# Two groups' transposes moved to the DMA queue in a fused retention and feed-forward kernel, with a state update placed earlier and the last output cut in two

## The chip, the cores and the metric

The kernel runs on one core of one Trainium2 chip. The metric is the device time of one execution in microseconds (us). A core has five engines that run side by side, each through its own instructions in order: TensorE (PE in the profile, with its weight loads shown apart as PEld), VectorE (DVE), ScalarE (ACT), GpSimd (POOL) and SyncE (SP). SP computes nothing here: it issues the DMAs that bring inputs in, take outputs away and transpose tiles, one after the other, and 16 DMA engines carry them out.

## The reference

Two stages follow each other. The first is retention: attention without a softmax, whose scores are damped by the distance of the two positions, with one decay rate for each of 8 heads. The second is a feed-forward block on all 4608 tokens with the activation h·cos(h).

```
# q, k, v: (8 batches, 8 heads, 576 positions, 64), float32
scores = (1 / sqrt(64)) * q @ k^T
gamma  = 1 - 2 ** (-5 - head)
D[i,j] = gamma ** (i - j)  where i >= j, else 0
x      = (scores * D) @ v          # then to (4608 tokens, 512)
h      = x @ w_in                  # w_in: (512, 2048)
out    = (h * cos(h)) @ w_out      # w_out: (2048, 512)
```

## The kernel before, in words

**Groups.** The 4608 tokens are 36 groups of 128, numbered from 0, so the fourth group is group 3 and the seventh and eighth are groups 6 and 7. Nine groups are two batches; group 4 of every nine lies half in one batch and half in the next. Each group goes through these steps:

- `load(g)`: SP issues one DMA each for q, k and v (line 107), 256 KB each, in pieces of 256 bytes; a group that lies in two batches takes six DMAs of half the size.
- `prep(g)`: GpSimd multiplies q and k with powers of the decay and casts them to bf16 in the tile `qks` (lines 132 and 133), and casts v to `vb` (line 139). For group 3, k is done by VectorE, and the first four groups have v cast by ScalarE (line 158), behind a copy of their transposes.
- `transposes(g)`: `qks` turned by 128x128 blocks, into `qkT`. For groups below `N_PE_T` this is done by 8 TensorE instructions into PSUM (line 151) and two ScalarE copies out of it (line 156); for later ones it is one DMA that SP issues (line 146).
- `scores(g)`: 8 products of k and q (line 173), which need `qkT`, then masked by VectorE into `ret` (line 182).
- `state(g)`: 4 products of k and v that add to a running state (line 201), which need `qks` and `vb` but no transpose; VectorE brings it out as `sb` (line 210) for the next group.
- `attn_out(g)`: what the state gives (line 230) and what the scores give (line 243), summed in PSUM and evacuated to the tile `xT` (line 255).

**Blocks.** The feed-forward part runs in ten blocks n = 0 to 9 of 512, 256, 256 and then 512 tokens. In a block `mm1` makes h (line 270); ScalarE takes the cosine (line 278), VectorE the product (line 279). Then `mm2` multiplies with `w_out`, 16 instructions for each 128 tokens (line 287); ScalarE copies the result to `ot` (line 296) and SP issues its store (line 298).

**The order.** All orders are written out by hand. The attention work of later groups is put between the matmuls of `mm2` by the list `todo`: a pair (index, work) is done before the matmul of that index. `pair(6, "ab", 16, 27)` in block 1 means: state(6) before index 11, scores(6) and scores(7) before 16, state(7) before 21, attn_out of both before 27. Block 0's first `mm1` piece holds state(3) and attn_out(3) in its middle, before its fourth quarter.

After every store the function `feed(s)` (s is the output's group number) puts more work into the queues of SP and GpSimd: first the DMA transposes of the groups prepared by earlier feeds, then the loads of up to two more groups, then the preparation of up to two more. What a feed gives SP stands in SP's queue behind the store of s and ahead of the store of s + 1. Feed 0 loads groups 6 and 7; feed 1 loads 8 and 9; feed 2 issues the first DMA transpose (group 8) and loads 10 and 11; feed 3 issues the transposes of 9 and 10, feed 4 of 11 and 12, feed 5 of 13 and 14, and feeds 6, 7 and 8 of 15, 16 and 17. The loads of groups 4 and 5 wait for the second of the four `w_out` loads. Input tiles have 6 buffers each, `qks`, `vb` and `qkT` 8, and `ot` 4.

The last 128 tokens' output is cut by columns (`cols`), so that the first columns can be stored while the last are still computed.

Of the kernel before, what the change touches and what calls it, by code (L numbers as in the profile page):

```python
# [17 lines left out]
def kernel(  # L18
# [34 lines left out]
    widths = [512, 256, 256] + [512] * 7  # L53
    assert sum(widths) == NTOK
    starts = [sum(widths[:n]) for n in range(len(widths))]
    N_PE_T = 8

    consts = ctx.enter_context(tc.tile_pool(name="consts", bufs=1))
    first = ctx.enter_context(tc.tile_pool(name="first", bufs=1))
# [130 lines left out]
    def state(g):  # L190
        c = g % PER
        if c == PER - 1:
            return
        qks, vb, qkT, qT = tiles["a", g]
        fresh = c in (0, MIX)
        if fresh:
            tiles["stps"] = psum.tile([P, HG, P], F32, tag="st", name="st")
        ps = tiles["stps"]
        p0 = HP if c == MIX else 0
        for hg in range(HG):  # L200
            nc.tensor.matmul(  # L201
                ps[:, hg, :],
                lhsT=qks[p0:, 1, 2 * hg : 2 * hg + 2, :].rearrange("s h d -> s (h d)"),
                rhs=vb[p0:, 2 * hg : 2 * hg + 2, :].rearrange("s h d -> s (h d)"),
                start=(fresh and hg == 0),
                stop=(c in (MIX - 1, PER - 2) and hg == HG - 1),
                skip_group_check=True,
            )
        sb = stp.tile([P, HG, P], BF16, tag="sb", name="sb")
        nc.vector.tensor_tensor(  # L210
            out=sb,
            in0=ps,
            in1=diag2.unsqueeze(1).to_broadcast([P, HG, P]),
            op=ALU.mult,
        )
        tiles["sb", g + 1] = sb

    def attn_out(gs, bank, evac=nc.vector.tensor_copy):


        ps = psum.tile([P, len(gs), HG, P], F32, tag=bank, name="ov")
        for x, g in enumerate(gs):
            c = g % PER
            if c == 0:
                continue
            qT = tiles["a", g][3]
            sb = tiles.pop(("sb", g))
            n = HP if c == MIX else P
            for hg in range(HG):
                nc.tensor.matmul(  # L230
                    ps[:, x, hg, :n],
                    lhsT=sb[:, hg, :],
                    rhs=qT[:, hg, :n],
                    start=(hg == 0),
                    stop=False,
                    skip_group_check=True,
                )
        for x, g in enumerate(gs):
            vb = tiles.pop(("a", g))[1]
            ret = tiles.pop(("ret", g))  # L240
            for hg in range(HG):
                for he in range(2):
                    nc.tensor.matmul(  # L243
                        ps[he * D : he * D + D, x, hg, :],
                        lhsT=vb[:, 2 * hg + he, :],
                        rhs=ret[:, he, hg, :],
                        start=(g % PER == 0 and hg == 0),
                        stop=(hg == HG - 1),
                        skip_group_check=True,
                    )  # L250
        n = max(m for m in range(len(starts)) if starts[m] <= gs[0] * P)
        if ("x", n) not in tiles:
            tiles["x", n] = xp.tile([P, DG, 512], BF16, tag="xT", name="xT")
        t0 = gs[0] * P - starts[n]
        evac(  # L255
            tiles["x", n][:, :, t0 : t0 + len(gs) * P].rearrange("p c (x i) -> p x c i", i=P), ps
        )
# [23 lines left out]
    def mm2(n, tsi, et, c0=0, c1=DM):  # L281
        gT = tiles["g", n]
        if et == 0:
            bank = {0: "nmnm", 1: "nm", 2: "mn"}.get(n, "mnan")[tsi] if c0 == 0 else "ba"[c0 % DM // P % 2]
            tiles["o", tsi] = psum.tile([P, c1 - c0], F32, tag=bank, name="o")
        ps = tiles["o", tsi]
        nc.tensor.matmul(  # L287
            ps,
            lhsT=gT[:, et, tsi * P : (tsi + 1) * P],
            rhs=w_out_sb[:, et, c0:c1],  # L290
            start=(et == 0),
            stop=(et == ET - 1),
        )
        if et == ET - 1:
            ot = op.tile([P, c1 - c0], F32, tag="o", name="ot")
            nc.scalar.copy(ot, ps)  # L296
            s = starts[n] // P + tsi
            nc.sync.dma_start(out[s * P : (s + 1) * P, c0:c1], ot)  # L298
            feed(s)
# [98 lines left out]
    for g in range(G4):  # L398
        if g == 0:
            prep(1, early=True)  # L400
        w_dma += [load_w_in(e, e + 512) for e in ((0,), (512,), (1024, 1536), ())[g]]
        if g == 2:
            w_dma += [load_w_out(e, e + 4) for e in range(0, ET, 4)]
            load(4, gate=w_dma[5])
            load(5)
            nc.gpsimd.tensor_copy(tri_mix, tri)
            nc.gpsimd.memset(tri_mix[:HP, HP:], 0.0)
        if g + 1 < G4:
            state(g)
            transposes(g + 1, "nn", only=(1,))  # L410
            if g + 2 < G4:
                prep(g + 2, early=True)
            scores(g + 1, "ab"[(g + 1) % 2], idle=3)
            attn_out([g], "m", evac=nc.scalar.copy)
# [21 lines left out]
    for n, w in enumerate(widths):  # L436

        if n in (0, 3):
            halves = [(h, et) for et in range(0, ET, 4) for h in range(2)]
            if n == 3:  # L440
                halves.sort()
            blocks = [(et, half * 256, 256) for half, et in halves]
        elif n == 1:
            blocks = [(et, half * P, P) for half in range(2) for et in (0, 8)]
        else:
            blocks = [(et, 0, w) for et in range(0, ET, 1024 // w)]
        banks = {0: "abmabmab", 1: "amba", 2: "bmab", 3: "mamabmab"}.get(n, "abmabmab")
        for i, (et, c0, cw) in enumerate(blocks):

            inside = {  # L450
                (0, 0): {3: lambda: (state(3), attn_out([3], "m"))},
                (1, 0): {4: lambda: scores(5, "b")},
                (1, 1): {3: lambda: attn_out([5], "b", evac=nc.scalar.copy)},
            }.get((n, i), {})
            mm1(n, et, c0, cw, banks[i], inside)
            if (n, i) == (3, 1):
                late.pop()()

        g = starts[n] // P + w // P
        if n == 0:  # L460
            todo = [
                (45, lambda: transposes(4, "ab")),
                (49, lambda: state(4)),
                (50, lambda: scores(4, "a")),
                (57, lambda: attn_out([4], "a")),
                (61, lambda: transposes(5, "ba")),
                (63, lambda: state(5)),
            ]
        elif n == 1:
            todo = [(4, lambda: transposes(6, "mb")), (9, lambda: transposes(7, "mb"))]  # L470
            todo += pair(6, "ab", 16, 27)
        elif n == 2:
            todo = pair(g, "ab", 11, 24) + pair(g + 2, "ba", 31, 40)[:2]
            late += [lambda: (state(g + 3), attn_out([g + 2, g + 3], "b"))]
        elif n + 1 < len(widths):
            todo = [
                (5, lambda: state(g)),
                (12, lambda: scores2(g)) if n == 3 else (0, lambda: None),
                (25 if n == 3 else 20, lambda: (attn_out([g, g + 1], "m"), scores2(g + 2))),
                (16, lambda: state(g + 1)),  # L480
                (36, lambda: state(g + 2)),
                (52, lambda: (attn_out([g + 2, g + 3], "m"), scores2(g + 4))),
                (45, lambda: state(g + 3)),
            ]
        else:
            todo = []
        todo.sort(key=lambda u: u[0])
        order, cols = [], [(0, DM)]
        for tsi in range(w // P):
            if (n + 1, tsi + 1) == (len(widths), w // P):  # L490
                cols = [(0, DM // 2), (DM // 2, 3 * DM // 4), (3 * DM // 4, DM)]
            order += [(tsi, et, c0, c1) for c0, c1 in cols for et in range(ET)]
        if n == 0:

            part = 3 * ET // 4
            order[: 2 * ET] = [
                (tsi, et, 0, DM)
                for tsi, et in [(t, e) for e in range(part) for t in range(2)]
                + [(t, e) for t in range(2) for e in range(part, ET)]
            ]  # L500
        for i, (tsi, et, c0, c1) in enumerate(order):
            while todo and todo[0][0] <= i:
                todo.pop(0)[1]()
            mm2(n, tsi, et, c0, c1)
        assert not todo
# [30 lines left out]
```

## Time and profile before

| | us |
|---|---|
| median of 3 runs (310.72 to 311.67) | 311.48 |
| the profiled execution's own time | 310.72 |
| its span in the profile | 308.8 |
| PE busy | 302.1 (98%) |
| DVE busy | 176.1 (57%) |
| ACT busy | 116.7 (38%) |
| POOL busy | 97.2 (31%) |

The span goes from the first to the last instruction of the profiled execution; some 2 us of its own time lie around it. Busy shares are means over the whole span. Waits of an engine are listed with what released them, and the chain of work that ended last is followed back from the last instruction. TensorE's clock was at full speed throughout. For a DMA the duration in the list of instructions is that of its issue on SP; its transfer ends later, and the time from issue to landing is given apart. In parts of the profile, `qkT<-qks` is a DMA transpose and `tr` is the PSUM tile of a TensorE transpose.

### The profile page before, as it was taken

The page shows a single profiled execution, that of the slowest core. Times are in us where ns is not written, and L with a number is a line of the kernel's source. Part 1 is how long each engine was busy: PE and PEld are TensorE (multiplying, and loading weights), DVE is VectorE, ACT ScalarE, POOL GpSimd, SP SyncE. Part 2 cuts the span into 40 slices and gives each one's busy share as a digit, 9 for nine tenths or more (in the row PEclk, how much of TensorE's full clock was granted, in tenths as well). Part 3 has the DMA queues.
Part 4 walks back from the last instruction along what each step waited for, and adds up shares of the span by engine and source line. Part 5 has one row for each costly group of instructions (what it writes and reads, how often), then busy time and mean ns, then how long its engine had stood idle before and what let it go on. Part 6 is the DMA issues. An engine that isn't in the chain of part 4 may idle for free.

```text
span 308.8 us, 5686 instructions
## 1 busy us (share of the span) xinstructions
PE 302.1 (98%) x2361; PEld 171.2 (55%) x2361; DVE 176.1 (57%) x179; ACT 116.7 (38%) x136; POOL 97.2 (31%) x120
## 2 busy tenths in 40 slices
PE   8899999999999999999999999999999999999996
PEld 3478547857588554445544554455445544554444
DVE  5766424565777764755466556755576556724610
ACT  3566234615046212640264016511551056015611
POOL 2740066644563554452542244214430000000000
PEclk9999999999999999999999999999999999999999
DMA  8999999999999999999990999279935510110012
GB/s 212 210 210 207 202 227 217 213 225 209 196 235 203 234 219 218 227 196 198 239 244 3 213 214 228 28 166 227 232 59 70 136 37 0 36 68 34 2 65 71
DMA packets 148697, 49.65 MB, mean 161 GB/s; under 512 B 138688, under 2 KB 144192, under 8 KB 148672
## 3 DMA queue, kind: packets, MB, share of 16 engines
q1 hardware_dynamic: 144448, 45.10, 77.3%
q0 software_dynamic: 4224, 4.19, 8.2%
q8 instruction: 18, 0.29, 0.4%
q14 instruction: 7, 0.06, 0.1%
HBM read 36.70 MB, written 9.44 MB: 149 GB/s over the span
## 4 chain that ended last, share of the span: by engine, by line
PE 72%; DMA 11%; SPq 11%; POOL 3%; issue 1%; ACT 1%; DVE 0%; POOLq 0%; ACTq 0%
PE o L287 33%; PE h L270 31%; SPq L107 8%; DMA fq<-in_q_dram 5%; DMA fk<-in_k_dram 5%; PE ov L243 2%; PE sc L173 2%; PE st L201 2%; SPq L146 2%; PE ov L230 1%; DMA qkT<-qks 1%; POOL qks L133 1%; POOL qks L132 1%; SPq L298 1%; PE tr L151 0%
## 5 line engine op out<-in xcount | busy, mean ns | idle before, releaser
L287 PE MATMUL o<-w_out_sb,gT 128*128 128x512 bf16 (+2 forms) x608 | 134.8, 368 | 0.3 <-DVE ret L182 0.3
L270 PE MATMUL h<-xT,w_in_sb 128*128 128x512 bf16 (+2 forms) x832 | 127.6, 313 | 0.6 <-DVE xT L255 0.3
L279 DVE TENSOR_TENSOR gT<-h,cosh 128x1024 bf16<-128x1024 f32 x72 | 88.2, 1225 | 56.7 <-ACT cosh L278 56.6
L270 PEld LDWEIGHTS <-w_in_sb 128*128 128x128 bf16 x832 | 75.7, 98 | 51.2 <-issue 1.5
L278 ACT ACTIVATE cosh<-h,half_pi 128x1024 f32<-128x1024 f32 x72 | 80.2, 1113 | 52.1 <-PE h L270 52.1
L287 PEld LDWEIGHTS <-gT 128*128 128x128 bf16 x608 | 55.3, 98 | 56.8 <-issue 0.6
L132 POOL TENSOR_TENSOR qks<-fq,gq 128x512 bf16<-128x512 f32 x32 | 33.3, 1042 | 107.9 <-DMA fq<-in_q_dram 103.0
L296 ACT COPY ot<-o 128x512 f32<-128x512 f32 (+2 forms) x38 | 21.4, 563 | 120.6 <-PE o L287 117.6
L133 POOL TENSOR_TENSOR qks<-fk,gk 128x512 bf16<-128x512 f32 x35 | 36.5, 1042 | 13.5 <-DMA fk<-in_k_dram 12.2
L182 DVE TENSOR_TENSOR ret<-sc,tri 128x1024 bf16<-128x1024 f32 x32 | 38.0, 1218 | 3.6 <-PE sc L173 3.6
L210 DVE TENSOR_TENSOR sb<-st,diag_105 128x512 bf16<-128x512 f32 x32 | 22.0, 687 | 28.9 <-PE st L201 28.9
L255 DVE CAST xT<-ov 128x1024 bf16<-128x1024 f32 (+1 forms) x17 | 19.7, 1161 | 24.3 <-PE ov L243 24.3
L139 POOL CAST vb<-fv 128x512 bf16<-128x512 f32 x32 | 19.5, 610 | 7.8 <-DMA fv<-in_v_dram 5.9
L201 PEld LDWEIGHTS <-qks 128*128 128x128 bf16 (+1 forms) x128 | 9.3, 97 | 7.5 <-issue 1.3
L201 PE MATMUL st<-vb,qks 128*128 128x128 bf16 (+1 forms) x128 | 12.4, 219 | 0.1
L243 PE MATMUL ov<-ret,vb 128*64 128x128 bf16 x288 | 12.0, 222 | 0.0
L173 PEld LDWEIGHTS <-qkT 64*128 64x128 bf16 x288 | 8.1, 94 | 5.8 <-ACT qkT L156 2.3
L173 PE MATMUL sc<-qkT 64*128 64x128 bf16 x256 | 10.3, 217 | 0.3 <-DMA qkT<-qks 0.3
L230 PEld LDWEIGHTS <-sb 128*128 128x128 bf16 x128 | 8.3, 98 | 3.7
L156 ACT COPY qkT<-tr 128x512 bf16<-128x512 bf16 x12 | 6.6, 587 | 9.0 <-PE tr L151 9.0
L243 PEld LDWEIGHTS <-vb 128*64 128x64 bf16 x288 | 8.7, 109 | 2.0
L230 PE MATMUL ov<-qkT,sb 128*128 128x128 bf16 (+1 forms) x116 | 8.8, 215 | 0.0
(45 smaller groups left out, 53.5 us busy)
## 6 DMA issues: line engine op xcount, KB each, us to landing
out_dram<-ot SPq DMA_DIRECT2D x35, 256.0 KB, 4.1
fk<-in_k_dram SPq DMA_DIRECT2D x32, 256.0 KB, 4.9
fv<-in_v_dram SPq DMA_DIRECT2D x32, 256.0 KB, 4.9
fq<-in_q_dram SPq DMA_DIRECT2D x28, 256.0 KB, 4.1
w_in_sb<-in_moe_w_in_dram POOLq DMA_DIRECT2D x4, 512.0 KB, 8.9
w_out_sb<-in_moe_w_out_dram POOLq DMA_DIRECT2D x4, 512.0 KB, 16.1
fq_110<-in_q_dram SPq DMA_DIRECT2D x2, 512.0 KB, 4.4
fq<-in_q_dram SPq DMA_DIRECT2D x8, 128.0 KB, 4.1
```

What stands on the lines that cost most here:

```text
L107: i = nc.sync.dma_start(f[p0:p1], src[b, :, s0 : s0 + p1 - p0, :].rearrange("h s d -> s h d"))
L132: nc.gpsimd.tensor_tensor(out=qks[:, 0], in0=fq, in1=tq, op=ALU.mult)
L133: (nc.vector if g == 3 else nc.gpsimd).tensor_tensor(out=qks[:, 1], in0=fk, in1=tk, op=ALU.mult)
L173: nc.tensor.matmul(ps[:, he, hg, :], lhsT=qkT[d0 : d0 + D, HG + hg, :], rhs=qT[d0 : d0 + D, hg, :], start=True, stop=True,)
L182: nc.vector.tensor_tensor(out=ret.rearrange("p a b i -> p (a b) i"), in0=ps.rearrange("p a b i -> p (a b) i"), in1=mask.unsqueeze(1).to_br ...
L201: nc.tensor.matmul(ps[:, hg, :], lhsT=qks[p0:, 1, 2 * hg : 2 * hg + 2, :].rearrange("s h d -> s (h d)"), rhs=vb[p0:, 2 * hg : 2 * hg + 2, ...
L210: nc.vector.tensor_tensor(out=sb, in0=ps, in1=diag2.unsqueeze(1).to_broadcast([P, HG, P]), op=ALU.mult,)
L243: nc.tensor.matmul(ps[he * D : he * D + D, x, hg, :], lhsT=vb[:, 2 * hg + he, :], rhs=ret[:, he, hg, :], start=(g % PER == 0 and hg == 0), ...
L270: nc.tensor.matmul(ps[:, j, :], lhsT=w_in_sb[:, dg, (et + j) * P : (et + j + 1) * P], rhs=xT[:, dg, c0 : c0 + w], start=(dg == 0), stop=(d ...
L278: nc.scalar.activation(cosh, ps, ACTF.Sin, bias=half_pi, scale=1.0)
L279: nc.vector.tensor_mul(gT[:, et : et + m, c0 : c0 + w], ps, cosh)
L287: nc.tensor.matmul(ps, lhsT=gT[:, et, tsi * P : (tsi + 1) * P], rhs=w_out_sb[:, et, c0:c1], start=(et == 0), stop=(et == ET - 1),)
```

## The change

Three edits are made at once.

1. `N_PE_T` goes from 8 to 6: groups 6 and 7 are transposed by DMA. The two entries of block 1's `todo` that held their TensorE transposes (before indices 4 and 9) go, and `pair(6)` is placed at 14 and 26 in place of 16 and 27: state(6) before index 9, scores before 14, state(7) before 20, attn_out before 26. In SP's queue the transpose of group 6 now stands in feed 1, behind the store of output 1 and ahead of the loads of groups 8 and 9; that of group 7 stands in feed 2, ahead of group 8's, behind the store of output 2 and ahead of the loads of groups 10 and 11.
2. state(3) is no longer in the middle of block 0's first `mm1` piece; it stands ahead of that piece, right behind attn_out(2). attn_out(3) stays where it was.
3. The last output's columns are computed in parts of 256 and 256, in place of 256, 128 and 128.

```diff
-    N_PE_T = 8
+    N_PE_T = 6
...
     def mm2(n, tsi, et, c0=0, c1=DM):
...
-            bank = {...}.get(n, "mnan")[tsi] if c0 == 0 else "ba"[c0 % DM // P % 2]
+            bank = {...}.get(n, "mnan")[tsi] if c0 == 0 else "b"
...
+        state(g)
         if g + 1 < G4:
-            state(g)
             transposes(g + 1, "nn", only=(1,))
...
-                (0, 0): {3: lambda: (state(3), attn_out([3], "m"))},
+                (0, 0): {3: lambda: attn_out([3], "m")},
...
         elif n == 1:
-            todo = [(4, lambda: transposes(6, "mb")), (9, lambda: transposes(7, "mb"))]
-            todo += pair(6, "ab", 16, 27)
+            todo = pair(6, "ab", 14, 26)
...
-                cols = [(0, DM // 2), (DM // 2, 3 * DM // 4), (3 * DM // 4, DM)]
+                cols = [(0, DM // 2), (DM // 2, DM)]
```

More of the change, by code (lines that the diff above doesn't have):

```diff
@@ L283, in mm2 @@
         if et == 0:
-            bank = {0: "nmnm", 1: "nm", 2: "mn"}.get(n, "mnan")[tsi] if c0 == 0 else "ba"[c0 % DM // P % 2]
+            bank = {0: "nmnm", 1: "nm", 2: "mn"}.get(n, "mnan")[tsi] if c0 == 0 else "b"
             tiles["o", tsi] = psum.tile([P, c1 - c0], F32, tag=bank, name="o")
```

## The prediction

> **What bounds the kernel now.** I read the page's shares and slices first, then the chain that ended last, the waits, and the order of time on SP and PE where the chain leaves PE.
>
> PE is busy 98% of the span at full clock. The lower rows say more: the DMA engines are at nine tenths or more in the first 24 of 40 slices, and less after.
>
> ```profile
> PE 302.1 (98%) x2361; PEld 171.2 (55%) x2361; DVE 176.1 (57%) x179; ACT 116.7 (38%) x136; POOL 97.2 (31%) x120
> DMA  8999999999999999999990999279935510110012
> ```
>
> The chain in order of time (start, us, what) runs from about 50 to 117 us not over PE but over SP's issues, the DMAs and POOL, returns to PE at the scores of group 17, which wait for a DMA transpose, and is PE alone from there:
>
> ```profile
> 111.89 1.04 SPq L298
> 113.04 4.22 DMA qkT<-qks
> 117.30 0.40 PE sc L173 x8
> 117.70 2.70 PE o L287 x12
> ```
>
> In the list of waits that arrival costs PE's matmuls 0.3 us. So SP's stream and PE's own work come out level at 117.3 us: work put on either before that moves the end.
>
> SP's issues in order of time (start, us, instruction) show whether SP has slack there. From 31.6 to 134.7 us it never idles for over 0.3 us, and stores wait behind other work: the store at 89.54, output 5, was ready at 85.06+0.58 = 85.6. The distance from store to store is the price of what a feed holds:
>
> ```profile
> 49.60 1.02 SPq L298 DMA_DIRECT2D out_dram<-ot  x1
> 57.40 1.31 SPq L298 DMA_DIRECT2D out_dram<-ot  x1
> 58.81 1.39 SPq L146 DMA_TRANSPOSE qkT<-qks  x1
> 66.09 2.60 SPq L298 DMA_DIRECT2D out_dram<-ot  x1
> 78.68 0.57 SPq L298 DMA_DIRECT2D out_dram<-ot  x1
> 79.36 3.85 SPq L146 DMA_TRANSPOSE qkT<-qks  x2
> 89.54 0.64 SPq L298 DMA_DIRECT2D out_dram<-ot  x1
> 90.30 4.04 SPq L146 DMA_TRANSPOSE qkT<-qks  x2
> 100.38 1.08 SPq L298 DMA_DIRECT2D out_dram<-ot  x1
> ```
>
> A store and six loads take 7.80 us with no transpose (49.60 to 57.40), 8.69 with one (to 66.09), 10.86 and 10.84 with two.
>
> On PE, block 1's mm2 holds the work that is removed; idle time would stand in brackets and there is none.
>
> ```profile
> 58.84 0.61 PE L151 MATMUL tr<-ident,qks 128*128 128x128 bf16 x8
> 59.29 1.24 PE L287 MATMUL o<-w_out_sb,gT 128*128 128x512 bf16 x5
> 60.37 0.61 PE L151 MATMUL tr<-ident,qks 128*128 128x128 bf16 x8
> 60.81 0.59 PE L287 MATMUL o<-w_out_sb,gT 128*128 128x512 bf16 x2
> 62.65 0.62 PE L173 MATMUL sc<-qkT 64*128 64x128 bf16 x16
> ```
>
> For the moved state(3), engines in order of time around 18 us: the cast of group 3's v starts only when its load has landed, and PE fills that time with the first h matmuls.
>
> ```profile
> 17.82 1.48 PE L270 MATMUL h<-xT,w_in_sb 128*128 128x256 bf16 x12
> 18.09 0.62 ACT L158 CAST vb<-fv 128x512 bf16<-128x512 f32 x1 [1.33 <-DMA fv<-in_v_dram]
> 19.14 0.39 PE L201 MATMUL st<-vb,qks 128*128 128x128 bf16 x4
> 20.91 0.81 PE L270 MATMUL h<-xT,w_in_sb 128*128 128x256 bf16 x6 [0.27 <-DVE xT L255]
> ```
>
> **What the Trainium skill says.** "DMA: Bandwidth & Descriptors", section Anatomy of one DMA: a DMA's semaphore wait is done by the issuing sequencer before dispatch, so a transpose and whatever it waits for stand in front of SP's later loads; SP's unbroken row of issues agrees. The same page, section Issuing engines are not separate DMA queues: all DMAs share the 16 engines. So a transpose costs the loads engine time besides SP's; the rising distances agree. Its section Latency and other measured facts gives DMA transposes 261 GB/s, or 350 to 400 when contiguous; 256 KB is then an estimated 0.7 to 1.0 us of engine time, less than the 1.3 us that SP spends on one issue (median 1308 ns of 28). "TensorE: Matmul & The Clock Gate", part 4, gives a PE transpose 275 to 390 ns; here eight take 59.29-58.84 = 0.45 us, 56 ns each, so the measured price is used.
>
> **The change part by part.**
>
> *PE transposes.* Removed: 8 at 0.45 us, 8 at 60.81-60.37 = 0.44, together -0.89 us of PE, and four ScalarE copies of 0.59 that PE doesn't wait for.
>
> *DMA transposes.* Two more issues on SP before 117 us. Feed 1 goes from none to one: 8.69-7.80 = +0.89. Feed 2 goes from one to two: 10.85-8.69 = +2.16. Sum +3.05 us; I take 3.05. The lower bound is twice 0.89 = 1.8, the upper twice 2.16 = 4.3; the bare issues, 2 x 1.35, give 2.7. Everything that stands behind on SP comes later by this: the loads of groups 8 on, hence POOL's preparations, hence all transposes up to group 17's. Neither transpose waits for POOL: group 6 is prepared by 48.6, group 7 by 52.1+1.0 = 53.1, and their turns on SP come at about 50.7 and 59.7.
>
> *Where PE feels it first: scores(7).* Feed 2 starts at 57.40+0.89 = 58.3; its store takes 1.3, so the transpose of 7 is issued at 59.7 and, at the 4.0 us to landing of group 8's, lands at 63.7. PE without any stall would reach scores(7) at 57.98 + 14 matmuls of 0.22 + state(6) 0.22 + scores(6) 0.28 = 61.5, plus 0.95 from state(3) below: 62.5. So PE waits some 1.2 us there. From there 18 o matmuls (3.9), state(7) 0.22 and attn_out 1.1 bring it to 69.1, where before they ended at 68.1: PE is then about 1 us late.
>
> *Next: scores(11).* Its transpose, issued at 79.36, landed 4.9 us later, at 84.27; PE needed it at about 84.36. Now it lands at 87.3, and PE, 1 us late, waits some 2 us more: PE is then as late as the stream, about 3.0.
>
> *Scores(17).* Landing was at 117.26 and becomes 120.3. PE arrives about 0.3 earlier, as before, so the 3.05 reaches PE in full. After it every landing has room: the transpose of 18 was issued at 118.3 and needed at 139.8. SP had idle time from 134.7 to 138.5, which takes up the lateness of its stream, but PE has no idle time from which to recover. Stores that are late by 3 us hold up no copy: `ot` has four buffers, and output 8's copy at 105.0 needs store 4, issued at 78.68.
>
> *State(3) earlier.* It needs the cast that ends at 18.71. PE reaches it at 17.89 instead of after 12 h matmuls, so it waits 0.9 us in front of those matmuls, which hid that wait before. Then 0.3 for the state, 1.42 for h, 0.67 for attn_out(3): ov ends at about 21.2 and not 20.2. DVE's `sb` (0.69) now runs during the h matmuls and no longer ahead of `xT`, which gives 0.1 back, and h goes on at 21.85 instead of 20.91. That is +0.95 us of PE, between 0.7 and 1.1. It lies ahead of the wait at scores(7), so the wait shrinks by as much; without that cover it would cost the end 0.95. Store 0, at 40.77, moves some 0.2; the DMA engines have loads queued then, so I count nothing.
>
> *Last output.* Matmuls: 16 of 256 columns took 304.23-302.48 = 1.75 us, the two parts of 128 took 0.93+0.90 = 1.83: -0.08. The last copy has 256 columns, 0.37 instead of 0.27: +0.10. The last store is 128 KB instead of 64, 1.7 instead of 1.6 to landing: +0.1. Nothing lies behind it: +0.1.
>
> Sum: 3.05+0.1 = +3.15 us. The -0.89 and +0.95 fall into waits. Against the profiled execution's own 310.72 (308.8 of it span) this gives 313.9; that execution was the fastest of three, 0.76 below the median, so the median of the runs becomes 311.48+3.15 = 314.6.
>
> **Rivals.**
>
> *The transposes are hidden.* While SP spends 1.3 us on a transpose, the DMA engines still work off loads queued ahead, and the loads behind it issue in 0.57 instead of 1.3. If the stream lost less than some 0.8 us, PE's own sum would decide: -0.89+0.95+0.1 = +0.16, 311.6 and no change. For it: feed 2's single transpose cost only 0.89. Against: the pairs cost 3.05 over none, and the DMA engines run empty around them (two digits in the answer for that feed fall to 1 and 0).
>
> *The transposes cost more.* Two in a row had up to 2.3 and 2.6 us of issue, against 1.3. If both new ones cost the full step of 2.16, the stream is 4.3 late: 311.48+4.3+0.1 = 315.9; and if group 7's lands late enough for PE to be later than the stream, more.
>
> *PE gains.* If group 17's wait weren't real and state(3) found its v ready, -0.89+0.1-0.1 = -0.9, 310.6. Against: the stream would also have to lose nothing.
>
> **How the numbers follow.** The stream 2.2 to 4.0 late: 0.65, giving 313.8 to 315.6, and 314.6 as the forecast. Hidden: 0.13. More: 0.18. A gain: 0.04. The range leaves out most of the hidden case and the far end of the dear one: 312.7 to 316.2. A difference of 0.3%, 0.93 us, is about what a measurement of this kernel can tell from none: slower 0.85, same 0.11, faster 0.04.
>
> **What would show it.** In the profile after: store-to-store distances on SP of about 8.7 and 10.9 in feeds 1 and 2; PE waiting for `qkT` at the scores of groups 7 and 11, 3 us in sum, and at 17; PE waiting for `vb` near 18 us; a chain that still leaves PE for SP up to about 120. Wrong: if scores(17) start before 118.5, or if PE is late again after 121.

## The result and the profile after

The changed kernel takes 314.75 us (median of 5 runs, 314.05 to 315.43) against 311.48 (median of 5, 310.62 to 311.94): +3.27 us, a ratio of 1.0111 with a 95% interval of [1.0084, 1.0139]. It is slower, beyond the 0.3% that a measurement can tell. The forecast was 314.6. Here and below the differences in us are those of medians of all executions, while a ratio leaves out those in a slower state (over 1.5% above the fastest of the same kernel) and isn't the ratio of the two medians. The profiled execution was one of the longer of the five, 315.26 us with a span of 313.4, so its own differences sum to +4.5 and not +3.3.

The chain of the changed kernel that ended last (start, us, what), at the two places where it returns from a DMA transpose to PE:

```profile
82.12 6.15 DMA qkT<-qks
88.31 0.40 PE sc L173 x8
...
116.90 4.28 DMA qkT<-qks
121.22 0.40 PE sc L173 x8
121.62 2.69 PE o L287 x12
```

The scores of group 17 start at 121.22 where they started at 117.30: +3.92 us. After that the chain is PE alone, as before. Between the two places it isn't the stream's alone: it runs over PE from 88.31 to 108.75 and comes back to SP through the copy and the store of output 7. So in this profile PE and the stream are late by almost the same, and experiments have to part them. SP's issues of the same execution, in order of time (start, us, instruction), without its loads (`x2` is two issues in a row):

```profile
49.80 0.95 SPq L298 DMA_DIRECT2D out_dram<-ot  x1
50.85 1.39 SPq L146 DMA_TRANSPOSE qkT<-qks  x1
59.60 1.10 SPq L298 DMA_DIRECT2D out_dram<-ot  x1
60.80 2.72 SPq L146 DMA_TRANSPOSE qkT<-qks  x2
70.11 1.09 SPq L298 DMA_DIRECT2D out_dram<-ot  x1
```

Feed 1 now takes 59.60-49.80 = 9.80 us (7.80 before), feed 2 takes 10.51 (8.69 before). The stream is 4.0 us late at store 3 and 3.86 at the transpose of group 17 (116.90 against 113.04).

PE's waits in the list of waits (who, on what: us in sum, times, longest), and PE in order of time with the idle time before an instruction in brackets:

```profile
PEld L173 <- DMA qkT<-qks: 3.3, 3, 2.3
PE sc L173 <- DMA qkT<-qks: 2.6, 2, 2.1
PE st L201 <- ACT vb L158: 0.8, 1, 0.8
```

```profile
18.71 0.38 PE L201 MATMUL st<-vb,qks 128*128 128x128 bf16 x4 [0.84 <-ACT vb L158]
...
64.69 0.40 PE L173 MATMUL sc<-qkT 64*128 64x128 bf16 x8 [2.13 <-DMA qkT<-qks]
...
121.22 0.40 PE L173 MATMUL sc<-qkT 64*128 64x128 bf16 x8 [0.51 <-DMA qkT<-qks]
```

One thing was not in the forecast: TensorE's clock. In these stretches of the changed kernel the figure behind the busy times of the five engines (PE, PEld, DVE, ACT, POOL) is the granted clock as a share of full speed; behind it stand the DMA engines' share and GB/s:

```profile
62.00:64.60 2.60, 0.57 (x10) 0.23 (x8) 1.23 (x1) 0.00 (x0) 1.75 (x3) 1.00 1.17 208
66.00:68.00 2.00, 2.00 (x10) 0.90 (x8) 0.97 (x2) 0.25 (x1) 0.74 (x1) 0.50 1.17 231
68.00:70.00 2.00, 2.00 (x13) 1.02 (x11) 0.08 (x1) 0.00 (x0) 1.34 (x2) 0.67 1.21 223
```

After the wait of 2.13 us PE ran at half clock from about 66 to 69 us. What is left of block 1 from 65.02 to 72.02, 18 o matmuls, state(7) and attn_out, took 7.0 us; by the durations before it is 3.92+0.22+1.11 = 5.25, so the half clock cost some 1.7 us.

It did not come in every execution. The mean clock of each is on record: 0.995 and 0.994 in the two longest of the five, 315.26 (the profiled one) and 315.43, and 1.0 in the other three, 314.05, 314.29 and 314.75. Their median is 2.8 us above the kernel before. So most of the loss is there without the half clock, which adds about 1 us where it comes; five executions are few for this figure.

### The profile page after: what moved, and what is told of

The parts are those of the page before. It is cut to its first block, busy times and chain, and to the rows that moved or that the text cites. A ratio compares the mean times of both kernels' runs of the same rounds, so it can differ in the third digit from the quotient of the medians.

```text
span 313.4 us, 5618 instructions
## 1 busy us (share of the span) xinstructions
PE 302.8 (97%) x2329; PEld 170.5 (54%) x2329; DVE 176.3 (56%) x179; ACT 114.7 (37%) x131; POOL 97.3 (31%) x120
## 4 chain that ended last, share of the span: by engine, by line
PE 74%; DMA 13%; SPq 9%; POOL 2%; issue 1%; ACT 1%; DVE 0%; POOLq 0%; ACTq 0%
PE h L270 35%; PE o L287 31%; DMA fq<-in_q_dram 7%; SPq L107 7%; DMA qkT<-qks 3%; DMA fv<-in_v_dram 2%; PE ov L243 2%; PE sc L173 2%; PE st L201 2%; PE ov L230 1%; POOL qks L132 1%; SPq L146 1%; SPq L298 1%; POOL qks L133 1%; ACT ot L296 0%
## 5 line engine op out<-in xcount | busy, mean ns | idle before, releaser
L287 PE MATMUL o<-w_out_sb,gT 128*128 128x512 bf16 (+1 forms) x592 | 135.9, 377 | 0.3 <-DVE ret L182 0.3
L296 ACT COPY ot<-o 128x512 f32<-128x512 f32 (+1 forms) x37 | 21.3, 576 | 126.9 <-PE o L287 122.1
L156 ACT COPY qkT<-tr 128x512 bf16<-128x512 bf16 x8 | 4.5, 588 | 8.8 <-PE tr L151 8.8
```

The costliest lines, as they stand in the source:

```text
L287: nc.tensor.matmul(ps, lhsT=gT[:, et, tsi * P : (tsi + 1) * P], rhs=w_out_sb[:, et, c0:c1], start=(et == 0), stop=(et == ET - 1),)
```

## The experiments

Theory A is the prediction's: the two more transposes make SP's stream late, and PE meets the stream at the scores of groups 7, 11 and 17. Theory D is that PE's own lateness counts: the wait at the scores of 7, the half clock after it and the state update come to 0.84 - 0.89 + 2.13 + 1.7 = 3.8 us, as much as the stream's. The profile after can't tell them apart. Each run is compared with runs of the kernel before on the same chip. Their medians are 311.43 for the single edits and the two spare transposes; 312.25 for the later scores, group 7 alone and the two with ScalarE's stores; 311.63 for feed 1 alone, the spare loads and the earlier start; 312.12 for the last. Profiles are of single executions, and times in them are set against the one profile of the kernel before.

**Each edit alone.** The first edit alone:

```diff
-    N_PE_T = 8
+    N_PE_T = 6
-            todo = [(4, lambda: transposes(6, "mb")), (9, lambda: transposes(7, "mb"))]
-            todo += pair(6, "ab", 16, 27)
+            todo = pair(6, "ab", 14, 26)
```

> The kernel before with the first edit alone: groups 6 and 7 transposed by DMA, their scores at index 14. Theory A (SP's stream sets the end: two more transposes make everything behind them on SP late by 3 to 4 us): the whole loss is here, +3.0 to +3.7 us, since the state update's wait lies ahead of the wait at the scores of group 7 and only makes that one shorter. Theory B (the edits add up, each with its own loss): +3.3 less 0.85 for the state update and 0.1 for the last output, some +2.3 us. In the profile A expects PE to wait about 3 us for the transpose of group 7, where the changed kernel waited 2.1.

Measured: 315.15 us, +3.72, ratio 1.0117 [1.0095, 1.0139]. The whole loss is here. PE waited 2.9 us at the scores of group 7, as theory A said, and 2.1 in the changed kernel, where state(3) has made it late already:

```profile
64.66 0.61 PE L173 MATMUL sc<-qkT 64*128 64x128 bf16 x8 [2.88 <-DMA qkT<-qks]
```

But this execution doesn't speak for theory A alone. The granted clock was half from 63.8 to 70.6 us, and PE then waited for no later transpose: its chain is nearly all PE from 64.66 on, and at group 17 it and the landing (issued at 117.43, 4.2 us) come together. Its mean clock, 0.988, was the lowest of six; the two executions at 0.999 took 314.74 and 314.75, +3.3.

The second edit alone:

```diff
+        state(g)
         if g + 1 < G4:
-            state(g)
...
-                (0, 0): {3: lambda: (state(3), attn_out([3], "m"))},
+                (0, 0): {3: lambda: attn_out([3], "m")},
```

> The kernel before with the second edit alone: state(3) ahead of block 0's first mm1 piece. Theory A: PE waits 0.84 us for the cast of group 3's v and is 0.85 us late from there; at the scores of group 17, where it had 0.3 us to wait, that takes up 0.3, so the end moves by +0.5 us (0.2%). Theory B: the full +0.85. Rival C (covered anyway): 0.

Measured: 311.65 us, +0.22, ratio 1.0013 [0.9997, 1.0028]. The full 0.85 (1.0027) lies just inside the interval, as does 0, so this run doesn't tell the three expectations apart.

The third edit alone:

```diff
-                cols = [(0, DM // 2), (DM // 2, 3 * DM // 4), (3 * DM // 4, DM)]
+                cols = [(0, DM // 2), (DM // 2, DM)]
```

> The kernel before with the third edit alone: the last output's columns in parts of 256 and 256. Worked out from the profile: +0.1 us for the longer last copy, +0.1 for the larger last store, -0.05 for the matmuls: between 0 and +0.2 us. Rival: the profile after has 0.73 us more between the last copy's start and the end of the span than the one before; if that is the edit's, +0.7 us.

Measured: 311.62 us, +0.19, ratio 1.0014 [0.9990, 1.0039]: no difference that can be told. From the last copy's start to the end of the span it is 309.6-306.57 = 3.0 us in this profile, 2.7 before, 3.5 after, and 3.1 with the first edit alone, whose last output is that of before; so the 0.73 between before and after isn't all the edit's.

**The stream without PE's part.** Two more DMA transposes at the same places in SP's queue, read by nobody, with TensorE's transposes kept:

```diff
+        if s in (1, 2):
+            spare = trp.tile([P, 2 * HG, P], BF16, tag="spare", bufs=1, name="spare")
+            qks = tiles["a", s + 5][0]
+            nc.sync.dma_start(spare, qks.rearrange("s m h d -> s (m h d)"), transpose=True)
         while transposed < min(prepared, s + 10):
```

> The kernel before with two more DMA transposes at the places where the changed kernel has them in SP's queue, of the same data but into a spare tile that nobody reads; TensorE still transposes groups 6 and 7, and nothing waits for the new ones. So SP's stream is loaded as in the changed kernel and PE's own work is as before. Theory A: the stream is 3 to 4 us late, and PE meets it at the scores of groups 11 and 17: +3.0 to +3.7 us. Rival D (PE's late arrival is what counts: the wait at the scores of group 7, the state update and the half clock after the wait, 3.7 us in sum): +0 to +0.5 us.

Measured: 315.30 us, +3.87, ratio 1.0141 [1.0108, 1.0174]. PE of this run in order of time:

```profile
84.51 0.40 PE L173 MATMUL sc<-qkT 64*128 64x128 bf16 x8
88.00 0.40 PE L173 MATMUL sc<-qkT 64*128 64x128 bf16 x8 [3.09 <-DMA qkT<-qks]
...
121.25 0.40 PE L173 MATMUL sc<-qkT 64*128 64x128 bf16 x8 [0.87 <-DMA qkT<-qks]
```

PE meets the late stream only at groups 11 and 17, its clock stays full, and the scores of 17 start at 121.25, as in the changed kernel. This execution took 315.01 us; in the other five the mean clock was 0.989 to 0.995, and they took 314.90 to 318.32. So the stream is enough for the whole loss, without PE's own additional waits and without a half clock. Whether PE's lateness would be enough without the stream's no run shows, since none took the lateness from the stream; and PE's wait at the scores of 7 is itself the stream's work.

**The wait at group 7 taken away.** The changed kernel with

```diff
-            todo = pair(6, "ab", 14, 26)
+            todo = [
+                (9, lambda: state(6)), (14, lambda: scores(6, "a")), (20, lambda: state(7)),
+                (22, lambda: scores(7, "b")), (29, lambda: attn_out([6, 7], "a")),
+            ]
```

> The changed kernel with the scores of group 7 moved from index 14 to 22 of block 1 and attn_out of groups 6 and 7 from 26 to 29; SP's queue is the same. PE should wait 0.3 us or less there, not 2.1, and keep its full clock. Theory A (SP's stream sets the end by itself): the wait only moves to the scores of groups 11 and 17, and the end stays where the changed kernel has it, +3.0 to +3.9 us over the kernel before. Theory D (the wait at the scores of group 7 and the half clock after it set the end): the end falls to +1.0 us over the kernel before or less.

Measured: 316.99 us, +4.74, ratio 1.0139 [1.0097, 1.0181]. Theory D said that the end falls when the wait at 7 goes: the wait is gone and the loss is not. PE in order of time:

```profile
88.34 0.40 PE L173 MATMUL sc<-qkT 64*128 64x128 bf16 x8 [3.11 <-DMA qkT<-qks]
88.67 0.39 PE L287 MATMUL o<-w_out_sb,gT 128*128 128x512 bf16 x1
88.90 5.32 PE L270 MATMUL h<-xT,w_in_sb 128*128 128x256 bf16 x32
```

The wait moved to group 11. The 32 h matmuls after it took 5.32 us; the changed kernel took 3.68 for the same 32. So the half clock followed the wait and cost 1.6 us, now past the point where a later wait would have covered it: the scores of 17 found their transpose landed, and came at 122.3. All six executions of this run had a mean clock of 0.989 to 0.995. In the changed kernel the half clock lies ahead of the meeting at group 11 and so costs less.

**One transpose of the two.** Only group 7 by DMA:

```diff
-    N_PE_T = 8
+    N_PE_T = 7
-            todo = [(4, lambda: transposes(6, "mb")), (9, lambda: transposes(7, "mb"))]
-            todo += pair(6, "ab", 16, 27)
+            todo = [(4, lambda: transposes(6, "mb"))]
+            todo += pair(6, "ab", 15, 26)
```

> The kernel before with only group 7 transposed by DMA (group 6 by TensorE), without the other two edits; its scores at index 15. One more transpose in SP's stream, in feed 2, where the step from one to two measured 2.16 us in the kernel before. Theory A at half dose: +1.6 to +2.2 us. If the two transposes' cost were in feed 1 alone (9.80 there after the change, against 7.80), +0.3.

Measured: 312.65 us, +0.40, ratio 1.0012 [0.9994, 1.0030]; all 14 executions had full clock. Theory A at half dose, +1.6 to +2.2, was wrong. In the profile the store of output 3 was issued at 68.25, 2.16 us later than before, just the step that was expected, but the store of output 4 at 79.48, only 0.80 later: feed 3, which before held a store issue of 2.60 us, took up the rest. And the spare transpose in feed 1 alone (`if s == 1` in place of `if s in (1, 2)`):

> The kernel before with one more DMA transpose, of group 6 into a spare tile that nobody reads, in feed 1 alone; TensorE's work unchanged. With both it was +3.9 us, with one in feed 2 (group 7 by DMA) +0.4. If costs add, this one is +3 us or more; if one transpose is mostly taken up by the stream and only two are not, +0.5 to +1.5. The stream's store-to-store distance in feed 1 should be 9.8 us as in the changed kernel, against 7.80.

Measured: 314.59 us, +2.96, ratio 1.0103 [1.0074, 1.0131]. PE at the scores of 17, first in the run with group 7 alone, then in the run with feed 1 alone:

```profile
118.33 0.40 PE L173 MATMUL sc<-qkT 64*128 64x128 bf16 x8 [1.11 <-DMA qkT<-qks]
```

```profile
120.58 0.40 PE L173 MATMUL sc<-qkT 64*128 64x128 bf16 x8 [0.85 <-DMA qkT<-qks]
```

So 1.0 us late with the one, 3.3 with the other, 3.9 with both. By the medians it is 0.40, 2.96 and 3.87. The 1.0 is hardly more than chance: the third edit alone, whose code is that of before up to the last output, has these scores at 117.86 in its profile, 0.56 late. The sum is about right, but the shares are the other way round from the prediction's, which had 2.16 for feed 2 and 0.89 for feed 1. Why the earlier one is dearer isn't settled. Feed 1 took 10.4 us in this run, and one load in it had an issue of 2.67 us, where its neighbours had 1.0 and 1.2; issues of 2 to 3 us stand here and there in every run's stream (before: 2.12 at 46.0 us, 2.60 at 66.1), and what causes them the runs don't show.

**Is it the transposing?** Two plain loads of k in place of the two spare transposes:

```diff
+        if s in (1, 2):
+            spare = trp.tile([P, H, D], F32, tag="spare", bufs=1, name="spare")
+            t0 = (s + 6) * P - S
+            nc.sync.dma_start(spare, k[1, :, t0 : t0 + P, :].rearrange("h s d -> s h d"))
```

> The kernel before with two more plain loads of k, 256 KB each in pieces of 256 bytes, into a spare tile that nobody reads, at the places where the changed kernel has its two transposes. It prices the DMA engines' work against a transpose's own kind. If a transpose costs the stream what a load of its size costs, the stream and the end are as late as with two transposes, +3.9 us; from the distances of the kernel before, a load takes about 1.2 us, so I expect +2.0 to +2.6.

Measured: 314.98 us, +3.35, ratio 1.0107 [1.0080, 1.0134], which overlaps with the two transposes' 1.0108 to 1.0174. My +2.0 to +2.6 was too low. SP spent 0.43 us on issuing each of these loads and 1.3 to 1.4 on each spare transpose, so neither the transposing nor SP's own issue time is what is paid for. What is left is the work given to the DMA engines, of which a load of 256 KB in small pieces makes about as much; on SP it shows in the issues that follow (the transpose of group 8, behind the second spare load, took 2.27 us and not 1.39).

The bytes give a part of the price. Feed 1 moved 1.79 MB at a mean of 229 GB/s before, and 2.08 MB at 212 GB/s in the changed kernel; the 0.29 MB more are an estimated 1.3 us of the 2.0. The rest is a lower rate: between the transpose's issue and its landing it fell to 17 GB/s in one slice of 0.25 us, as it did between those of group 8's transpose in the kernel before. Feed 1 with a spare load in the transpose's place (2.09 MB, 225 GB/s, 9.30 us) has no such hole in that stretch.

**SP relieved, the engines not.** Two runs tried to speed the stream up without taking bytes from it. The changed kernel with an earlier start:

```diff
-            load(4, gate=w_dma[5])
+            load(4, gate=w_dma[4])
```

> The changed kernel with the loads of groups 4 and 5 waiting for the first of the four w_out loads and not for the second, so that SP's stream starts some 2.5 us earlier, at about 29 us and not 31.9, with the same DMAs in it. Theory A, if the stream has only a late start: all its landings come 2 us or more earlier and the end is +1 to +2 us over the kernel before. If the DMA engines' work sets the stream's pace (they have no idle time at 29 us, and the weights only come later instead): no better than +3, or worse where PE waits for w_out.

Measured: 315.33 us, +3.70, ratio 1.0115 [1.0084, 1.0146]. SP in order of time:

```profile
29.11 1.96 SPq L107 DMA_DIRECT2D fq<-in_q_dram  x2
31.11 2.31 SPq L107 DMA_DIRECT2D fk<-in_k_dram  x2
33.46 4.12 SPq L107 DMA_DIRECT2D fv<-in_v_dram  x2
37.63 0.62 SPq L107 DMA_DIRECT2D fq<-in_q_dram  x1
```

It starts 2.8 us earlier, its first issues take longer beside the weights, and by group 5 it stands at 37.63, where the changed kernel stood at 37.57. The other run is the first edit alone with the stores issued by ScalarE, with the kernel before as its control:

```diff
-            nc.sync.dma_start(out[s * P : (s + 1) * P, c0:c1], ot)
+            nc.scalar.dma_start(out[s * P : (s + 1) * P, c0:c1], ot)
```

> The first edit alone (groups 6 and 7 by DMA), with all stores of the output issued by ScalarE and none by SP. Some 1 us of issue for each of nine stores leaves SP's stream ahead of group 17's transpose; the DMA engines move the same bytes. Theory A, if the stream's lateness is SP's issue time: the stream is 3 us or more earlier at the scores of 7, 11 and 17, the waits go, and the end is at or below the kernel before, -1 to +0.5 us. If the stream is bound by the DMA engines' work and not by SP: no better than +2.5. ScalarE's cosines may be held up by its DMA issues; that would show as PE or VectorE waiting for them.

> The control: the kernel before with all stores issued by ScalarE. PE's work is as before; only the 0.3 us of wait at the scores of group 17 can be won: 0 to -0.5 us, or a loss where ScalarE's DMA issues hold up its cosines.

Measured: 322.10 us with the first edit (+9.85, ratio 1.0296 [1.0267, 1.0325]), 316.18 for the control (+3.93, 1.0123 [1.0092, 1.0153]). The gain failed in both. What held was the other branch of each: no better than +2.5 with the first edit, and a loss by what ScalarE's issues hold up in the control. Without its stores SP came to the transpose of 17 at 116.1, against 117.4 with them (the first edit alone); the transposes' issues grew instead, to 5.11 us for the pair of feed 2, against 2.96. ScalarE of the run with the first edit shows the price:

```profile
74.22 0.35 ACTq L298 DMA_DIRECT2D out_dram<-ot  x1
74.62 0.59 ACT L296 COPY ot<-o 128x512 f32<-128x512 f32 x1 [7.71 <-DMA fk<-in_k_dram]
```

The `ot` copy before this store ended at 66.9; the store was issued at 74.22, and the next copy, with the cosines after it, stood behind it on ScalarE for 7.7 us. With the plain loads and the earlier start this points to a stream that goes at the pace of the DMA path behind SP, not of SP's queue. That is argued and not shown, since PE and ScalarE were late themselves in the two runs with ScalarE's stores; which part of the path sets the pace wasn't tried.

**Other loads moved back.** The first edit alone with the later scores of 7 and

```diff
-        while loaded < min(NG, 2 * s + 8, s + 13):
+        while loaded < min(NG, 2 * s + 8 - (s == 3), s + 13 - (s >= 6)):
```

> The first edit alone, with two things that take the lateness away where PE meets it: the scores of group 7 at index 22 and attn_out of 6 and 7 at 29 (as in the run with later scores), and loads that aren't needed yet moved behind the transposes that are: group 13's from feed 3 to feed 4, and from feed 6 on each feed loads one group less far ahead, so that group 19's loads stand behind group 17's transpose. The same DMAs in all, in another order. Theory A: the loss of the first edit (+3.7 us) goes for the most part, as PE waits about 1 us at the scores of 7 and not at all at 11 and 17, and gains 0.9 from its transposes: +0.2 to +1.2 us over the kernel before. If PE's own order were the cause, or if a late load then holds up SP at a transpose that waits for its preparation, +2.5 us or more.

Measured: 316.35 us, +4.23, ratio 1.0114 [1.0056, 1.0172]. PE in order of time:

```profile
66.25 0.40 PE L173 MATMUL sc<-qkT 64*128 64x128 bf16 x8 [1.82 <-DMA qkT<-qks]
...
112.93 0.40 PE L173 MATMUL sc<-qkT 64*128 64x128 bf16 x8 [2.02 <-DMA qkT<-qks]
```

The waits at 11 and 17 went, as meant, and one at the scores of group 15 came in their place, since the loads moved back now stood ahead of its transpose. The profiled execution, 314.71 us, and one other had full clock; the other four, at 0.989 to 0.995, took 316.27 to 317.62, so the median holds half clock besides. This doesn't speak against the stream, but the expected gain was not had, and the run doesn't prove that a stream in time brings the loss back. No run beat the kernel before.

## Why the prediction was right

*The level at 117 us* held, and with it the mechanism: work added to the stream ahead of it moved the end, be it transposes that nobody reads (+3.9 us) or no transposes at all (+3.4). It wasn't true of every item: the one transpose more in feed 2 moved the median by 0.40, which can't be told from nothing.

*The sum* was right, +3.15 for +3.27; the parts of its main term were not. The step "feed 1 goes from none to one: 8.69-7.80 = +0.89" measured 9.80-7.80 = 2.00, and in the seven profiles with a transpose there and the stores on SP feed 1 took 9.8 to 10.4 us. The step "feed 2 goes from one to two: +2.16" measured 10.51-8.69 = 1.82, and alone, as said, it hardly moved the end. In sum 3.8 in place of 3.05 in the profile, 3.86 at the transpose of 17. The steps took differences of single distances for prices, and the middle one, 8.69, was a low one: in the profile of the third edit alone, with the same code in this stretch, the distances with no, one and two transposes are 8.05, 10.17 and 10.99. In the very profile that was used, feed 0, with a store, six loads and no transpose, took 49.60-40.77 = 8.83, more than feed 2 with one. The sum doesn't contain the middle distance, as 0.89+2.16 = 10.85-7.80 (10.99-8.05 = 2.94 in the other profile), and so it held. That a feed with two less a feed with none also prices one transpose in each of two feeds was luck. In this profile the rival "the transposes cost more", 4.3, was nearer; the median of the runs, +3.27, is nearer to the forecast.

*Scores(7)* were to wait 1.2 us and waited 2.13: feed 1 was 1.1 longer than said, so the transpose of 7 was issued at 60.8 and not 59.7. *PE some 1 us late after block 1* was wrong: its h matmuls began at 72.02 where they began at 68.31, +3.7. Of the 2.7 beyond the forecast 0.9 is the longer wait and 1.7 the half clock, which the prediction didn't have; without it, as in three of the five executions, PE comes out some 2 us late by this sum. So *scores(11)*, said to wait 2 us, waited some 0.3 in this profile. The end hardly felt the mistake, because the stream was as late as PE by then; that the two were so near was luck.

*State(3)* was right: 0.84 of wait for the cast (the prediction's own figures give 18.71-17.89 = 0.82 where it says 0.9), and h went on at 21.75 where it went on at 20.91. It was covered by the later wait, as said: that wait is 2.13 us with it and 2.88 without it. Alone it could not be told from nothing.

*The last output* was sized at +0.1; alone it measured +0.19, with an interval that holds 0.

*Hidden transposes* needed a stream that lost under 0.8 us. With group 7 alone that nearly holds, +0.40 and no difference that can be told; with group 6 in feed 1 it fails. *PE gains* failed with it: the 0.89 us were saved and then waited away.

*A reading* was off: SP does idle once for over 0.3 us between 31.6 and 134.7, for 0.55 us ahead of the store at 89.54. The argument doesn't change by it.

## What to carry to other kernels

A transpose moved from a busy TensorE to a DMA is not free where loads already fill the DMA path: here two of them cost about what two loads of 256 KB cost in the same places, and what stands behind them was late by up to that. How much of it reaches the end depends on the place, +3.0 us for feed 1 and +0.4 for feed 2. Look for the landing that comes level with the compute engine (here PE waited 0.3 us for it): it makes the whole queue ahead of it part of the critical path, though PE is 98% busy. Price an added item by several like places and more than one profile, since one store-to-store distance can be off by a microsecond.

## What the runs showed of the hardware

A wait of 2 to 3 us of PE can bring a stretch at half clock: 3.4 us of it in the profiles of the changed kernel (a wait of 2.1 us), the earlier start (3.2) and the later scores (3.1), and 6.8 us, twice as long, with the first edit alone (2.9), where it set in before the wait ended. It did not come in the profiled executions of the two spare transposes (3.1 us at the scores of 11), one spare transpose (3.0) and the spare loads (2.8), though others of the same kernels had a mean clock of 0.989 to 0.995: five of six, three of six and three of five. So one code meets it in some executions and not in others. The Trainium skill, "TensorE: Matmul & The Clock Gate", section Why this matters for your kernels, advises against idle gaps of more than about 3 us; here 2.1 was enough in the profiled execution. What else decides isn't shown.

A DMA issued by ScalarE while SP's stream filled the DMA path held ScalarE up to 7 us; what it waited for in that time the trace doesn't settle. The skill's "DMA: Bandwidth & Descriptors", section Issuing engines are not separate DMA queues, says that a second issuing engine saves only the sequencer's issue time; here SP's stream won 1.4 us at the transpose of 17 with nine stores gone from it, and the wait moved to an engine that had other work.
